# A listed order for all engine queues, one GpSimd operation moved, and idle products in the early gaps of TensorE

## The chip, the cores and the metric

One core of one Trainium2 chip runs the whole program. The metric is the device time of one execution in microseconds (us), the median of three timed runs; less is better. One more execution was recorded by the hardware profiler; every row below is from it.

## The reference

Gated linear attention feeds a channel-mixing layer, all in float32. Per batch (4) and head (8), over 768 steps, with 48 values per head:

```python
for t in range(S):
    state = alpha[:, :, t, :, None] * state + np.einsum('bhd,bhe->bhde', k[:, :, t], v[:, :, t])
    y[:, :, t] = np.einsum('bhd,bhde->bhe', q[:, :, t], state)
x = y.transpose(0, 2, 1, 3).reshape(B, S, H * D)          # 4 x 768 x 384
xk = mu_k * x + (1.0 - mu_k) * x_prev                     # x_prev: one step earlier
xr = mu_r * x + (1.0 - mu_r) * x_prev
k = np.maximum(xk @ w_k, 0.0)                             # 384 -> 1024
v = k * k @ w_v                                           # 1024 -> 384
r = 1.0 / (1.0 + np.exp(-(xr @ w_r)))
return (r * v)
```

## The kernel before

**Attention.** The 4 x 768 steps are cut into 24 chunks of 128, two chunks to a group `a` (12 groups). For a group, VectorE (DVE) forms running products of alpha with three scans `forth{a}.p`, multiplies q by them (`qP`), takes reciprocals (`turn`), runs three scans backwards (`back`) and multiplies k (`kP`). GpSimd (POOL) keeps the end values in between (`ends`: a copy to `pends`, a scaled copy to `pe`), and `turn` waits for them. For chunk `i`, TensorE (PE) transposes k (`trans`, tile `pt`), ScalarE (ACT) copies it out (`ht`), and PE multiplies: `enter{i}` (update of the state, scores) and `visit{i}` (outputs of the chunk), or, from `visit4` on, both in one job, `visit{i}` with the update and scores of chunk `i+1`. DVE masks the scores (`mask`) and advances the state (`state`), ACT and DVE move the outputs into `xt` (`leave`, `cross`).

**Channel mix.** Groups are joined to 7 column blocks `g` (two of 256 columns, five of 512). For each, the mix with the step before (`scale`, `blend`, `high`, `low`: a value is split into a rounded part and a remainder, so that three products in the fast float32 format give full accuracy), then on PE eight `up{g}.f` jobs of 9 matmuls, three `gate{g}.m`, and `down{g}.m.quarter`, four pieces of 6 matmuls for each of three output rows. ACT and DVE turn an up product into squares (`relu`, `square`, `whole`, `rest`).

**Weights** are loaded as packed words and split by ACT and DVE in the first 57 us: `top` (ACT, tile `tops` or `early`), `join` (DVE), `high` (ACT), `low` (DVE), for `k0` to `k3`, `r0`, `r1`, `v0` to `v3`. `down0.m.2` and `.3` need `v2` and `v3`.

**Order.** Everything that is added to the plan is a job with an engine, a cost in us and its needs. `Plan.order` tries 60 priority lists, keeps the shortest by its own costs, and the jobs are then issued in that order; each engine works its own queue strictly in that order. SyncE (SP) issues the transfers, and it too waits in its queue: a transfer whose data are not ready holds up those behind it. Three things lie outside the plan: 20 matmuls on zeros at the start, idle products (dummies) on zeros in front of the first real job of PE, and the operation `nu = 1 - mu` on POOL, issued ahead of all jobs. A dummy is one matmul of 112 columns, which the profile records as two.

```python
    todo = plan.order(sizes, ROUNDS)
    POOL.tensor_scalar(nu, mu, -1.0, 1.0, op0=ALU.mult, op1=ALU.add)
    at = WARMED
    cold = True
    for j in todo:
        if plan.eng[j] == "PE":
            if cold and at == WARMED:
                for i in range(int((plan.start[j] - at) / 0.19)):
```

Of the kernel before, what the change touches and what calls it, by code (L numbers as in the profile page):

```python
# [20 lines left out]
ALU = mybir.AluOpType  # L21
# [21 lines left out]
NT = 3  # L43
# [10 lines left out]
ROUNDS = 60  # L54
# [12 lines left out]
class Plan:  # L67
# [3 lines left out]
    LAG = {"PE": 0.25, "SP": 2.1, "DVE": 0.10, "ACT": 0.10, "POOL": 0.12}  # L71

    def __init__(self):
        self.eng, self.dur, self.fn, self.name, self.lag = [], [], [], [], []
        self.need = []
        self.first, self.users = {}, {}

    def add(self, eng, dur, fn, need=(), takes=(), uses=(), name="", lag=None):
# [3 lines left out]
        self.dur.append(dur)  # L82
        self.fn.append(fn)
# [31 lines left out]
    def run(self, pre, suc, key, free):  # L115

        n = len(self.eng)
        left = [len(d) for d in pre]
        ready = [0.0] * n
        start = [0.0] * n  # L120
        free = dict(free)
        wait = {e: [] for e in free}
        can = {e: [] for e in free}
        for j in range(n):
            if not left[j]:
                heapq.heappush(wait[self.eng[j]], (0.0, j))
        done = 0
        while done < n:
            best = None
            for e in free:  # L130
                if can[e]:
                    t = free[e]
                elif wait[e]:
                    t = max(free[e], wait[e][0][0])
                else:
                    continue
                if best is None or t < best[0]:
                    best = (t, e)
            t, e = best
            while wait[e] and wait[e][0][0] <= t:  # L140
                _, j = heapq.heappop(wait[e])
                heapq.heappush(can[e], (key[j], j))
            _, j = heapq.heappop(can[e])
            start[j] = t
            end = free[e] = t + self.dur[j]
            done += 1
            for k, lag in suc[j].items():
                ready[k] = max(ready[k], end + lag)
                left[k] -= 1
                if not left[k]:  # L150
                    heapq.heappush(wait[self.eng[k]], (ready[k], k))
        return start, max(s + d for s, d in zip(start, self.dur))

    def order(self, sizes, rounds):
# [3 lines left out]
        tail = [0.0] * n  # L158
        start, _ = self.run(pre, suc, list(range(n)), self.FREE)
        for j in sorted(range(n), key=lambda j: -start[j]):  # L160
            tail[j] = self.dur[j] + max((lag + tail[k] for k, lag in suc[j].items()), default=0.0)
        rng = random.Random(7)
        zero = {e: 0.0 for e in self.FREE}
        best = None
        key = [-x for x in tail]
        for r in range(rounds):
            start, span = self.run(pre, suc, key, self.FREE)
            if best is None or span < best[0]:
                best = (span, start, key)
            if r % 4 == 3:  # L170
                width = rng.choice((1.0, 2.0, 4.0, 8.0))
                key = [k + rng.uniform(-width, width) for k in best[2]]
            else:
                back, total = self.run(suc, pre, [-(s + d) for s, d in zip(start, self.dur)], zero)
                key = [total - b - d for b, d in zip(back, self.dur)]
        self.span, self.start = best[:2]
        return sorted(range(n), key=lambda j: (best[1][j], j))


# [1061 lines left out]
```

## Time and profile before

| | |
|---|---|
| median of 3 timed runs | 348.07 us (348.06 to 348.72) |
| profiled execution, its own time | 346.2 us |
| its span, first to last instruction | 344.5 us |
| busy: PE, DVE, ACT, POOL | 320.7, 221.1, 197.3, 20.4 us |
| mean granted clock of PE | 0.95 of full speed |

A timeline row gives start, length, engine, line, operation and tiles (out<-in), the count when like instructions follow each other, and in brackets how long the engine idled just before and what ended that. A clock of 1.00 is 2.4 GHz, 0.50 is 1.2 GHz. Matmuls are pipelined, so lengths of neighbouring PE rows overlap. Lines are those of the kernel before; in the changed kernel the same code stands 12 to 16 lines lower.

### The profile page before, as it was taken

The page shows a single profiled execution, that of the slowest core. Times are in us where ns is not written, and L with a number is a line of the kernel's source. Part 1 is how long each engine was busy: PE and PEld are TensorE (multiplying, and loading weights), DVE is VectorE, ACT ScalarE, POOL GpSimd, SP SyncE. Part 2 cuts the span into 40 slices and gives each one's busy share as a digit, 9 for nine tenths or more (in the row PEclk, how much of TensorE's full clock was granted, in tenths as well). Part 3 has the DMA queues.
Part 4 walks back from the last instruction along what each step waited for, and adds up shares of the span by engine and source line. Part 5 has one row for each costly group of instructions (what it writes and reads, how often), then busy time and mean ns, then how long its engine had stood idle before and what let it go on. Part 6 is the DMA issues. An engine that isn't in the chain of part 4 may idle for free.

```text
span 344.5 us, 10124 instructions
## 1 busy us (share of the span) xinstructions
PE 320.7 (93%) x4345; PEld 273.4 (79%) x4345; DVE 221.1 (64%) x421; ACT 197.3 (57%) x367; POOL 20.4 (6%) x60
## 2 busy tenths in 40 slices
PE   8546599999899999999999999999999999999992
PEld 8445599999798888888888888888888888888781
DVE  4979899896899537599337698264795212933010
ACT  4547799395378933199823299712398611987100
POOL 6100001020001002010001100000000000000000
PEclk9755599999999999999999999999999999999997
DMA  7797675324542035432035422043400001100011
GB/s 280 274 335 256 216 230 154 104 74 125 173 123 71 1 108 142 143 87 62 0 107 147 144 85 58 0 118 91 148 32 12 2 13 44 63 0 1 3 61 38
DMA packets 17204, 35.54 MB, mean 103 GB/s; under 512 B 3584, under 2 KB 7808, under 8 KB 17152
## 3 DMA queue, kind: packets, MB, share of 16 engines
q1 hardware_dynamic: 17008, 34.81, 33.0%
q8 instruction: 36, 0.59, 0.7%
q14 instruction: 16, 0.13, 0.1%
q10 hardware_dynamic: 144, 0.00, 0.0%
HBM read 26.55 MB, written 4.72 MB: 91 GB/s over the span
## 4 chain that ended last, share of the span: by engine, by line
PE 70%; DMA 9%; DVE 9%; ACT 7%; issue 2%; POOL 1%; SPq 1%; ACTq 0%; DVEq 0%
PE pm L847 24%; PE pm L810 24%; PE pm L835 9%; PE yu L485 3%; PE yu L513 3%; DMA xt<-xt 2%; PE sp L497 2%; DMA early<-wk_p 2%; DMA al<-al_p 2%; DMA mu<-mu_p 2%; PE pt L468 2%; ACT x L790 2%; DVE pp L409 2%; PE sp L535 1%; PE yu L535 1%
## 5 line engine op out<-in xcount | busy, mean ns | idle before, releaser
L810 PE MATMUL pm<-xkh,wkh 128*128 128x512 f32 (+1 forms) x168 | 43.8, 370 | 1.5 <-ACT xkh L796 1.5
L810 PE MATMUL pm<-xkh,wkl 128*128 128x512 f32 (+1 forms) x168 | 42.8, 364 | 0.0
L810 PE MATMUL pm<-xkl,wkh 128*128 128x512 f32 (+1 forms) x168 | 42.6, 362 | 0.0
L847 PE MATMUL pm<-kb,wvh 128*128 128x512 f32 x120 | 42.1, 402 | 0.0
L790 ACT ACTIVATE x<-xt,mu 128x512 f32<-128x512 f32 (+1 forms) x42 | 25.2, 654 | 28.0 <-DMA xt<-xt 28.0
L847 PE MATMUL pm<-kha,wvh 128*128 128x512 f32 (+1 forms) x108 | 38.4, 355 | 0.0
L847 PE MATMUL pm<-kla,wvh 128*128 128x512 f32 (+1 forms) x108 | 37.0, 342 | 0.0
L847 PE MATMUL pm<-kha,wvl 128*128 128x512 f32 (+1 forms) x108 | 36.8, 341 | 0.0
L810 PEld LDWEIGHTS pm<-xkh,wkh 128*128 128x128 f32 x168 | 29.6, 193 | 6.8 <-ACT xkh L796 1.7
L810 PEld LDWEIGHTS pm<-xkh,wkl 128*128 128x128 f32 x168 | 29.9, 193 | 5.0
L816 ACT ACTIVATE r<-pm 128x512 f32<-128x512 f32 (+1 forms) x56 | 29.5, 530 | 7.6 <-PE pm L810 6.9
L810 PEld LDWEIGHTS pm<-xkl,wkh 128*128 128x128 f32 x168 | 29.8, 192 | 4.9
L822 ACT ACTIVATE k<-r 128x512 f32<-128x512 f32 (+1 forms) x56 | 31.5, 565 | 3.2 <-DVE kla L825 2.3
L825 DVE TENSOR_TENSOR kb<-k,kb 128x512 fp32r<-128x512 f32 x20 | 13.9, 693 | 24.2 <-ACT kb L819 12.9
L969 DVE TENSOR_TENSOR sig<-pm,sig 128x512 f32<-128x512 f32 (+1 forms) x21 | 12.8, 613 | 24.8 <-PE pm L847 24.6
L582 DVE TENSOR_TENSOR am<-sp,mask 128x512 f32<-128x512 f32 x24 | 16.4, 683 | 17.8 <-PE sp L497 17.8
L793 DVE SCALAR_TENSOR_TENSOR x<-xt,nu,x 128x512 f32<-128x512 f32 (+1 forms) x42 | 26.4, 665 | 1.5 <-ACT x L790 1.3
L560 ACT COPY xt<-yu 112x512 f32<-112x512 f32 x24 | 13.9, 580 | 23.3 <-PE yu L535 21.8
L649 ACT COPY ht<-pt 128x384 f32<-128x384 f32 x24 | 16.3, 677 | 19.1 <-PE pt L468 18.9
L847 PEld LDWEIGHTS pm<-kb,wvh 128*128 128x128 f32 x120 | 22.6, 188 | 5.0
L365 DVE TENSOR_TENSOR_SCAN pp<-al,tiny 128x256 f32<-128x256 f32 x36 | 22.8, 675 | 4.8 <-DMA al<-al_p 4.8
L409 DVE TENSOR_TENSOR_SCAN pp<-al,pp 128x255 f32<-128x255 f32 x36 | 25.2, 736 | 0.5 <-DVE pp L402 0.2
(90 smaller groups left out, 604.6 us busy)
## 6 DMA issues: line engine op xcount, KB each, us to landing
v<-v_p SPq DMA_DIRECT2D x12, 400.0 KB, 4.6
al<-al_p SPq DMA_DIRECT2D x12, 384.0 KB, 3.3
q<-q_p SPq DMA_DIRECT2D x12, 384.0 KB, 3.8
k<-k_p SPq DMA_DIRECT2D x12, 384.0 KB, 3.7
out<-sig SPq DMA_DIRECT2D x15, 256.0 KB, 2.1
early<-wk_p SPq DMA_DIRECT2D x4, 768.0 KB, 6.3
early<-wv_p SPq DMA_DIRECT2D x4, 768.0 KB, 4.5
q<-q SPq DMA_DIRECT2D x24, 48.0 KB, 2.2
```

The lines of the kernel that those rows point to most:

```text
L365: DVE.tensor_tensor_scan(view(a, pps)[:, p], view(a, als)[:, p], tiny.to_broadcast([128, n]), initial=START, op0=ALU.mult, op1=ALU.max,)
L409: DVE.tensor_tensor_scan(pp[:, p, 0 : n - 1][:, ::-1], x, x, initial=pp[:, p, n - 1 : n], op0=ALU.mult, op1=ALU.bypass,)
L560: ACT.copy(x[:R].rearrange("r i (s t) -> r i s t", s=2), yu[:R, :, : NP * HC].rearrange("r s (i t) -> r i s t", i=NP),)
L582: DVE.tensor_tensor(ams[i % 2], sp[:, :, : NP * HC].rearrange("c j (p t) -> c j p t", p=NP), mask.unsqueeze(1).unsqueeze(1).to_broadcast([ ...
L649: ACT.copy(hts[(i + 1) % 2].rearrange("t (r i) -> t i r", i=NT), pt)
L790: ACT.activation(x, now, AF.Copy, scale=mu[:, i, t : t + 1])
L793: DVE.scalar_tensor_tensor(x, prev, nu[:, i, t : t + 1], x, op0=ALU.mult, op1=ALU.add)
L810: PE.matmul(pk, w[:, t, cols], x[:, t], start=part == 0 and t == 0, stop=part == 2 and t == NT - 1,)
L816: ACT.activation(r, pk, AF.Relu)
L822: ACT.activation(k2, r, AF.Square)
L835: PE.matmul(pg, w[t // 2][:, t % 2, cols], x[:, t], start=part == 0 and t == 0, stop=part == 2 and t == NT - 1,)
L847: PE.matmul(pv, w[f // 2][:, f % 2, cols], x, start=f == 0 and i == 0, stop=f == NF - 1 and i == 2,)
```

## The change

`Plan.order` and its search are gone. A list of all 1,079 jobs, `ORDER`, stands in the source, and `Plan.follow` issues them in it, working out a start for each from the costs; costs were altered too (SP's jobs now have an issue time and a separate transfer time), but they now set only those starts. `nu` becomes a job on POOL that needs `ends0`; it stands behind `ends1` in the list. Dummies fill 0.6 of each gap that the worked-out starts leave on PE until the first job that takes the third accumulator (`up0.2`): besides the 13 in front of `trans0`, as before, now 38 more, in this order: 5, 3, 6, 4, 3, 2 before `trans1`, `enter0`, `visit0`, `enter1`, `trans2`, `trans3`, then 5, 5 and 5 before `enter2`, `visit2` and `enter3`.

```diff
-ROUNDS = 60
+FILL = 0.6
+ISSUE = 0.42
...
-    def order(self, sizes, rounds):
+    def follow(self, sizes, order):
+
         self.rings(sizes)
         pre, suc = self.links()
         n = len(self.eng)
...
+        for j in todo:
+            t = self.FREE[self.eng[j]]
+            if j in behind:
+                t = max(t, start[behind[j]] + self.dur[behind[j]])
+            start[j] = max([t, *(end[i] + lag for i, lag in pre[j].items())])
+            end[j] = start[j] + self.dur[j]
+            if self.moved[j]:
+                end[j] = max(end[j], end[behind[j]] if j in behind else 0.0) + self.moved[j]
...
+        place = {j: i for i, j in enumerate(order)}
+        return sorted(range(n), key=lambda j: (start[j], place[j]))
...
+ORDER = """
+0 2 213 18 1 218 4 5 6 7 9 8 10 15 12 214 13 20 22 11 3 215 14 216 24 16 263 219 217 264 220 223 19 268 25 221
...
+"""
...
-            jb = add("DVE", dve(n) + 0.05, b_, need=[js], uses=[("x", xi), ("xt", g)], name=f"blend {tag}{g}.{t}")
+            jb = add("DVE", dve(n) + 0.05, b_, need=[js, weighed], uses=[("x", xi), ("xt", g)], name=f"blend {tag}{g}.{t}")
...
+    weighed = add(
+        "POOL", 0.3, lambda: POOL.tensor_scalar(nu, mu, -1.0, 1.0, op0=ALU.mult, op1=ALU.add),
+        need=[rescale[0][0]], name="nu",
+    )
...
-    todo = plan.order(sizes, ROUNDS)
-    POOL.tensor_scalar(nu, mu, -1.0, 1.0, op0=ALU.mult, op1=ALU.add)
+    todo = plan.follow(sizes, [int(x) for x in ORDER.split()])
...
-            if cold and at == WARMED:
-                for i in range(int((plan.start[j] - at) / 0.19)):
+            if cold:
+                gap = plan.start[j] - at
+                for i in range(int((gap if at == WARMED else FILL * gap) / 0.2)):
```

On DVE, around `kP1` (the product into `k_102`), before. The join of weight `k3` (`early<-early,tops_171`) stands ahead of it:

```order
L764 TENSOR_TENSOR wkl_156<-early,wkh_152 128x768
L570 TENSOR_TENSOR xt_178<-xt_178,sp 112x2x64 x2
L752 SCALAR_TENSOR_TENSOR early<-early,tops_171 128x768
L393 TENSOR_TENSOR k_102<-k_102,pp_100 128x768
L613 TENSOR_TENSOR st_132<-st_131,yu 112x192
L616 TENSOR_TENSOR st_133<-st_132,yu 112x192
L618 TENSOR_TENSOR st_133<-st_133,pe_143 112x192
L582 TENSOR_TENSOR am_177<-sp,mask 128x512
```

The same place on DVE in the changed kernel:

```order
L776 TENSOR_TENSOR wkl_156<-early,wkh_152 128x768
L408 TENSOR_TENSOR k_102<-k_102,pp_100 128x768
L628 TENSOR_TENSOR st_132<-st_131,yu 112x192
L631 TENSOR_TENSOR st_133<-st_132,yu 112x192
L633 TENSOR_TENSOR st_133<-st_133,pe_143 112x192
L597 TENSOR_TENSOR am_177<-sp,mask 128x512
L380 SCALAR_TENSOR_TENSOR pp_99<-al_97,tiny 128x256 x3
L764 SCALAR_TENSOR_TENSOR early<-early,tops_171 128x768
L585 TENSOR_TENSOR xt_178<-xt_178,sp 112x2x64 x2
```

The join moved behind `kP1`, `state1`, `mask1` and three scans of group 2, still ahead of `cross1` (`xt_178`).

On SP, before, around the loads of group 4 (`k_101` and `q_103` are its k and q). The gather of `pe` stands ahead of the load of q:

```order
L327 DMA k_101<-k_p 128x768
L444 DMA pe_143<-pe_143 48x1x1 x2
L327 DMA q_103<-q_p 128x768
L350 DMA v_105<-v_p 128x800
L579 DMA xt_178<-xt_178 16x3x256 x2
```

The same place on SP in the changed kernel:

```order
L341 DMA k_101<-k_p 128x768
L986 DMA out<-sig_195 128x256
L341 DMA q_103<-q_p 128x768
L364 DMA v_105<-v_p 128x800
L459 DMA pe_143<-pe_143 48x1x1 x2
L594 DMA xt_178<-xt_178 16x3x256 x2
```

The loads of q and v moved ahead of the gather, and a store came in between.

On PE, before, at the third piece of the first down product (`wvh_160` is weight `v2`). The piece follows the second one (`wvh_159`) at once:

```order
L847 MATMUL pm_72<-kha,wvh_159 128x256
L847 MATMUL pm_72<-kha,wvl_163 128x256
L847 MATMUL pm_72<-kla,wvh_159 128x256
L847 MATMUL pm_72<-kha,wvh_160 128x256
L847 MATMUL pm_72<-kha,wvl_164 128x256
```

The same place on PE in the changed kernel, where the last rows of `visit4` stand ahead of the piece:

```order
L550 MATMUL sp<-q_103,st_132 64x64
L550 MATMUL sp<-q_103,st_131 64x64
L512 MATMUL sp<-q_103,k_101 64x64 x16
L859 MATMUL pm_72<-kha,wvh_160 128x256
L859 MATMUL pm_72<-kha,wvl_164 128x256
```

`enter4` and the whole of `visit4` moved from within and behind the third down product to ahead of this piece.

## Rows read from the trace of the kernel before

**Rows 1.** Stretch, length; busy (count) by engine; PEclk; DMA share; GB/s.
```profile
57.50:338.50 281.00, 278.61 (x3643) 234.61 (x3641) 171.35 (x333) 157.77 (x293) 11.96 (x24) 1.00 0.25 72
```

**Rows 2.** Timeline of PE at 89 us: start, length, instruction, [idle before].
```profile
89.69 0.77 PE L485 MATMUL yu<-v,ht 64*64 64x48 f32 x29 [1.68 <-ACT ht L649]
```

**Rows 3.** The same columns as in 1, VectorE alone.
```profile
8.40:57.04 48.64, 45.02 (x83) 0.68 0.79 257
```

**Rows 4.** Timeline of VectorE up to 57 us.
```profile
8.40 0.18 DVE L402 RECIPROCAL pp<-pp 128x3 f32<-128x3 f32 x1 [1.37 <-POOL pe L383]
...
14.17 1.84 DVE L365 TENSOR_TENSOR_SCAN pp<-al,tiny 128x256 f32<-128x256 f32 x3
...
16.78 0.95 DVE L393 TENSOR_TENSOR q<-q,pp 128x768 f32<-128x768 f32 x1
17.65 0.34 DVE L613 TENSOR_TENSOR st<-st,yu 112x192 f32<-112x192 f32 x1
...
18.30 0.68 DVE L582 TENSOR_TENSOR am<-sp,mask 128x512 f32<-128x512 f32 x1
...
25.12 0.96 DVE L752 SCALAR_TENSOR_TENSOR early<-early,tops 128x768 uint32<-128x768 uint32 x1 [1.29 <-ACT tops L744]
...
31.87 0.48 DVE L570 TENSOR_TENSOR xt<-xt,sp 112x128 f32<-112x128 f32 x2
...
37.27 0.48 DVE L793 SCALAR_TENSOR_TENSOR x<-xt,nu,x 128x256 f32<-128x256 f32 x1 [0.93 <-ACT x L790]
...
54.55 0.76 DVE L825 TENSOR_TENSOR kla<-k,kha 128x256 fp32r<-128x256 f32 x2
55.22 1.82 DVE L764 TENSOR_TENSOR wvl<-early,wvh 128x768 fp32r<-128x768 f32 x2
```

**Rows 5.** Timeline of GpSimd.
```profile
7.68 0.20 POOL L1051 TENSOR_SCALAR nu<-mu 128x6 f32<-128x6 f32 x1 [1.62 <-DMA mu<-mu_p]
```

**Rows 6.** Timeline of PE up to 69 us.
```profile
7.40 2.72 PE L1058 MATMUL pm<-zero 112*112 112x112 f32 x26
12.66 0.72 PE L468 MATMUL pt<-ident,k 128*128 128x128 f32 x3 [2.53 <-DVE k L393]
...
15.11 0.97 PE L485 MATMUL yu<-v,ht 64*64 64x48 f32 x30
...
15.95 1.09 PE L497 MATMUL sp<-q,k 48*64 48x64 f32 x30
...
39.91 1.01 PE L810 MATMUL pm<-xkh,wkh 128*128 128x256 f32 x3 [1.53 <-ACT xkh L796]
...
57.48 0.28 PE L847 MATMUL pm<-kha,wvh 128*128 128x256 f32 x1
...
62.80 0.79 PE L485 MATMUL yu<-v,ht 64*64 64x48 f32 x30
...
64.09 0.39 PE L847 MATMUL pm<-kha,wvh 128*128 128x256 f32 x1
...
66.72 0.77 PE L485 MATMUL yu<-v,ht 64*64 64x48 f32 x15
...
68.86 0.55 PE L468 MATMUL pt<-ident,k 128*128 128x128 f32 x3
```

**Rows 7.** Stretches as in 1, for the clock of PE.
```profile
12.00:13.00 1.00, 0.34 (x3) 0.35 (x3) 1.00 (x2) 1.00 (x2) 0.00 (x0) 0.92 0.64 234
28.65:33.50 4.85, 4.85 (x131) 4.12 (x131) 4.49 (x9) 3.06 (x5) 0.48 (x1) 0.50 0.85 251
88.00:89.69 1.69, 0.01 (x1) 0.00 (x1) 1.62 (x7) 1.64 (x4) 0.00 (x0) 1.00 0.80 177
```

**Rows 8.** SyncE from 60 to 95 us: its waits, then its timeline.
```profile
SPq L444 <- POOL pe L383: 5.6, 1, 5.6
...
77.47 0.53 SPq L327 DMA_DIRECT2D q<-q_p  x1
```

**Rows 9.** Chain that ended last: start, length, engine, tile, line, count.
```profile
202.08 16.69 PE pm L810 x72
```

More of the change, by code (lines that the diff above doesn't have):

```diff
@@ L70, with add @@
     FREE = {"SP": 0.8, "DVE": 1.6, "ACT": 2.4, "POOL": 3.6, "PE": 1.6}
-    LAG = {"PE": 0.25, "SP": 2.1, "DVE": 0.10, "ACT": 0.10, "POOL": 0.12}
+    LAG = {"PE": 0.25, "SP": 1.9, "DVE": 0.10, "ACT": 0.10, "POOL": 0.12}
     def __init__(self):
         self.eng, self.dur, self.fn, self.name, self.lag = [], [], [], [], []
-        self.need = []
+        self.need, self.moved = [], []
         self.first, self.users = {}, {}
-    def add(self, eng, dur, fn, need=(), takes=(), uses=(), name="", lag=None):
+    def add(self, eng, dur, fn, need=(), takes=(), uses=(), name="", lag=None, moved=0.0):
         j = len(self.eng)
@@ L113, in links @@
         return pre, suc
[L115 to L152, printed above, removed]
-    def order(self, sizes, rounds):
+    def follow(self, sizes, order):
         self.rings(sizes)
@@ L157, in order @@
         n = len(self.eng)
[L158 to L177, printed above, removed]
+        assert sorted(order) == list(range(n))
+        last, behind, ahead = {}, {}, {}
+        for j in order:
+            e = self.eng[j]
+            if e in last:
+                behind[j] = last[e]
+                ahead[last[e]] = j
+            last[e] = j
+        left = [len(d) + (j in behind) for j, d in enumerate(pre)]
+        self.start = start = [0.0] * n
+        end = [0.0] * n
+        todo = [j for j in range(n) if not left[j]]
+        for j in todo:
[6 more added lines that the diff above has]
+                end[j] = max(end[j], end[behind[j]] if j in behind else 0.0) + self.moved[j]
+            for k in (*suc[j], *([ahead[j]] if j in ahead else [])):
+                left[k] -= 1
+                if not left[k]:
+                    todo.append(k)
+        assert len(todo) == n
+        self.span = max(end)
+        place = {j: i for i, j in enumerate(order)}
+        return sorted(range(n), key=lambda j: (start[j], place[j]))
 def mm(n):
-    return 0.013 + n / 2400.0 if n > 128 else 0.068
+    return n / 2240.0
 def dve(n, psum=False):
@@ L339, in fetch @@
             tag = x + str(half)
-            ids = [add("SP", move(128 * NT * n * 4), one, takes=[(x, a)], name=f"load {x}{a}")]
+            ids = [add("SP", ISSUE, one, moved=move(128 * NT * n * 4), takes=[(x, a)], name=f"load {x}{a}")]
             if direct:
-                ids.append(add("SP", 0.5, extra, takes=[(x, a)], name=f"load {x}{a} again"))
+                ids.append(add("SP", 2 * ISSUE, extra, moved=0.5, takes=[(x, a)], name=f"load {x}{a} again"))
             took[x] = ids
@@ L449, in attention_inputs @@
                 rescale[a].append(
-                    add("SP", 0.1, small, need=[end], uses=[("pe", a)], name=f"gather pe{a}")
+                    add("SP", 1.25, small, moved=0.05, need=[end], uses=[("pe", a)], name=f"gather pe{a}")
                 )
@@ L715, in attention_products @@
                     mv = add(
-                        "SP", 0.2, lambda a=a: spread(a), need=done[a], uses=[("xt", slot_of[a])], name=f"spread{a}"
+                        "SP", 1.25, lambda a=a: spread(a), moved=0.35, need=done[a], uses=[("xt", slot_of[a])], name=f"spread{a}"
                     )
```

26 lines of the change are left out of this document (12 added, 14 removed), and 39 rows, old and new, of the table ORDER.

## The prediction

> **What bounds the kernel now.** I read the stretches first, then each engine in order of time, then the waits, and the chain last. From 57.5 us on TensorE (PE) is busy 278.61 of 281.00 us [rows 1]: there the time is matmul work, and an order can only win back the 2.39 us in which PE idles. 1.68 of them are one wait at 88 us, for a transposed tile `ht` [rows 2]. What else can be won lies before 57 us.
>
> There VectorE (DVE) is the limit: from 8.40 to 57.04 us it is busy 45.02 of 48.64 us [rows 3], so it idles 3.62 us. Three waits make up most of what matters. At 8.40 its reciprocal has waited 1.37 us for GpSimd (POOL) [rows 4], because POOL had stood 1.62 us in `nu` until the transfer of `mu` landed [rows 5]. At 25.12 a join waited 1.29 us for ScalarE's (ACT) tile `tops`, and at 37.27 a blend 0.93 us for `x` [rows 4]. DVE's last weight remainders (`low v2`, `low v3`, line 764) run from 55.22 to 57.04 [rows 4]; the third piece of the first down product, `down0.0.2`, follows on PE at 57.48 [rows 6]. I take this point, M, as the milestone. Whatever PE has done beyond the old list when it passes M, and whatever time M moves, is the gain; behind it both kernels have the same matmuls to do.
>
> **The change, part by part, against the profile's own span of 344.5 us.**
>
> *`nu` behind `ends0`.* It removes the wait at 8.40. The reciprocal then needs the end values, which POOL takes while DVE multiplies `q` (0.95 us for such a product [rows 4]), so nearly all of 1.37 is saved: **1.3 us** for DVE. `nu` is then due only at the first blend, at 37.27 in the old trace, some 20 us after its new place behind `ends1`: no cost.
>
> *The new DVE list up to `low v3`.* Comparing the two lists, nothing leaves it and these jobs are moved in front: `forth3.1`, `forth3.2`, `rest0.6`, `rest0.7`, `cross3`, `qP3`, `turn3`, `state4`, `mask4`. Prices [rows 4]: two scans at 1.84/3 = 0.61 make 1.22; two `rest` 0.67 (54.55 to 55.22); `cross` 0.48; `qP` 0.87 (16.78 to 17.65); `state` 0.65 (17.65 to 18.30); `mask` 0.68 less the overlap, 0.60; the reciprocal 0.1. Sum **4.6 us** more ahead of M.
>
> *DVE's idle time.* The 1.29 us wait was a join that stood in front of `kP1` while its weight was still in transfer; the join now stands behind `kP1`, `mask1` and three scans, and its load now stands ahead of the gather of `pe` and the load of `v` that it was behind. The 0.93 us wait sat behind the chain `kP1`, `mask1`, `cross1`, transfer of `xt`; that chain now starts some 4 us earlier (1.3 from `nu`, 1.29 from the wait, 0.9 from the join itself, and `cross1` has two jobs less ahead of it), and two other jobs, `low r0` and `qP2`, stand before the blend. I take both as gone, 2.2 us; the bounds are 0 and all 3.62 us. So `low v3` ends at 57.04 - 1.3 + 4.6 - 2.2 = 58.1, `low v2` 0.9 earlier, and **M = 57.2** (bounds 55.8 and 59.4).
>
> *What PE has done at M.* The old list has none of chunk 4's products there, the new one all: `enter4`, 62.80 to 64.09, and `visit4`, 66.72 to 68.86 [rows 6], together 1.29 + 2.14 = **3.43 us**. Can PE be at M by 57.2? From its first up product (39.91) to M it needed 17.57 us [rows 6]; less `enter3`, which now comes earlier (1.29), plus 3.43, it needs 19.7, and 1.9 less if the first two up products don't run at half clock. So up products that begin by 39.4 do, and the chain above lets them begin near 36. PE waits at M, not DVE. Gain at M: 57.48 - 57.2 + 3.43 = **3.7 us**.
>
> *Dummies in the early gaps.* 38 more of the 112-column products. At full clock 13 of them take 2.72 us [rows 6], 0.21 each, 7.9 us in all, within gaps that PE has anyway. As DVE decides M, the clock itself gives nothing that is not counted; they cost only if they run at half clock (below). Before, the clock was 0.92 in the microsecond from 12 to 13 and then half: it fell after the dummies had ended at 10.12 and PE had idled 2.53 us to 12.66 [rows 6, 7]. That gap shrinks by the 1.3 us, and the next ones hold dummies. Through the idle 1.68 us at 88 us the clock stayed at 1.00 [rows 7]. I take it that the clock holds.
>
> Here a rule is weighed. PE was busy 4.85 of 4.85 us from 28.65 to 33.50, with `visit` and `enter` products alone, and the clock stayed at 0.50 (1.2 GHz) [rows 7]. The Trainium skill ("TensorE: Matmul & The Clock Gate", What's actually happening) says that the gate is set by how busy PE has recently been: half rate by default, released by sustained activity. By it this stretch should have brought the clock back, and the new, fuller early stage would be safe; by the row, the small products alone do not bring a lost clock back, so it hangs on the dummies. By the rule the sum stands; by the row a fall that happens lasts to the first up products, which is the second rival.
>
> *SyncE's queue.* Before, the gather of `pe` stood in SP's queue ahead of the load of `q` for group 4 and waited 5.6 us for POOL; the load went out at 77.47 [rows 8]. That delay runs through `qP4`, `kP4` and the next loads into the 1.68 us wait of PE at 89.69 [rows 2]. Now the loads of `q` and `v` stand ahead of that gather, so I count **1.7 us** back. Against it, visits 9 to 11 are moved up by 10 to 20 us, into the up products of group 2, and need loads and gathers sooner. The trace of before has no such place; the bound below is 0, the bound above as large as the old waits, 2.4. I take 0.4, near the low end, because each visit still has more than 10 us of other products between it and its predecessor's release of the buffers.
>
> Sum: 3.7 + 1.7 - 0.4 = **5.0 us**. The profiled span goes from 344.5 to 339.5, that execution's own time from 346.2 to 341.2. The median of the three timed runs, 348.07, lies 1.87 above the profiled one; I carry that over: **343.1 us**.
>
> **The rivals.**
>
> *DVE wins back no idle time.* New waits replace the two named ones, since a denser list in one order is more easily held up. Then M is 59.4, the gain there 57.48 - 59.4 + 3.43 = 1.5, and if the later waits also come back as large as before, the time is 348.07 - 1.5 = 346.6. For it: ACT and the weight loads are no faster than before, and the extra jobs depend on ACT's results.
>
> *The clock falls anyway; slower.* Place: the gaps between 11 and 36 us. From `trans0`, now near 11.3, to the end of `visit2` PE has four transposes at 0.72, 33 dummies at twice 0.21, and six `enter` and `visit` blocks at 1.93 (15.11 to 17.04 at half clock) [rows 6]: 2.9 + 13.9 + 11.6 = 28.4, so `visit2` ends at 39.7; five dummies (2.1) and `enter3` (1.9) put the first up product at 43.7 and M at 43.7 + 19.7 = 63.4. Gain: 57.48 - 63.4 + 3.43 + 1.3 = -1.2, that is 349.3. It decides where M passes 62.2. For it: the dummies fill only part of each gap. Against it: the dummies are spread over all of the gaps, and none of the idle stretches left is as long as the 2.53 us after which the clock fell.
>
> *TensorE's long stretch is not full.* Weight loads are busy only 234.61 of its 281.00 us [rows 1]; if order could close a tenth of the other 46.4, the time would be 4.6 less than forecast, 338.5. Against it: 72 matmuls of 512 columns take 16.69 us, 0.232 each, in one unbroken piece of the chain [rows 9], and no order changes their number. The Trainium skill ("Perfetto Trace Analysis", Identifying the Most-Contended Engine) calls matmul busy time a poor measure of headroom and the weight loads' share a good one; by that rule this rival holds, and the trace agrees only with the share, not with the room.
>
> **How the numbers follow.** The forecast, 343.1, gets 0.62; its own range is 341 to 345. DVE without its idle time, or half of it, near 346.6: 0.20. The clock falls, near 349.3: 0.12, of which a third stays within 0.2%. PE's stretch shrinks: 0.02; something else, either way: 0.04. 0.2% (0.7 us) is about what a measurement of this kernel can tell from no change. Faster by more than that takes the first two, the fourth and some of the rest: 0.83; within it 0.07; slower 0.10. The low end of the range is the forecast with all DVE idle gone (1.4 less) and no new waits and no old ones (1.1 less): 340.6. The high end takes in the first rival with something above it: 347.0.
>
> **What would show it.** Right: DVE's first reciprocal near 7.1; `kP1` ending near 23, ahead of the join that it stood behind; the first up product near 36, at clock 1.00; `visit4` before M, PE idle for 2 us or so in front of `down0.0.2` near 57; no wait of SP for POOL ahead of the load of group 4's `q`; PE unbroken from there to the end, and 512-column matmuls at 0.232. Wrong: clock 0.50 in the records between 13 and 36 us, M above 60, or a new wait of more than 2 us behind M, at a transpose or a visit that comes too early.

## The result, and the profile after

The changed kernel takes 343.77 us (median of 4 executions, 343.34 to 344.42), the kernel before beside it 348.39 us (348.06 to 348.83): a ratio of 0.986, 95% interval 0.983 to 0.989. A second comparison on another chip, told below, gave 342.57 us and a ratio of 0.983 (0.980 to 0.986). All ten executions together have a median of 343.1 us, the number that was forecast; the kernel before has 348.6 over 78 executions in all comparisons. Four more of its executions, beside e5 to e10, ran in a slower state and are left out of every median and ratio here. The gain is 5.5 us. But the two profiles stand only 2.3 us apart (own times 346.2 and 343.89, spans 344.5 and 342.2), so part of the forecast's way to its number must be wrong. The lines of the profile after are read with that in mind.

The page of the profile after, TensorE's clock in 40 slices of 8.6 us:

```profile
PEclk9999999699999999999999999999999999999997
```

The early slices are at 9, where [rows 7] had 0.50 (a second profile, a11, has an early fall, see there); the eighth slice, from 60 to 68 us, shows a 6. The stretches say the same (length; busy of PE, PE's weight loads, DVE, ACT, POOL; PEclk; DMA share; GB/s):

```profile
10.00:36.00 26.00, 20.55 (x545) 18.16 (x544) 25.25 (x48) 16.79 (x27) 4.45 (x6) 1.00 0.86 284
36.00:57.00 21.00, 18.91 (x355) 17.93 (x354) 19.03 (x39) 17.30 (x41) 1.13 (x2) 1.00 0.69 211
57.00:65.00 8.00, 6.25 (x28) 5.95 (x29) 7.61 (x14) 5.20 (x11) 0.00 (x0) 0.57 0.44 117
65.00:110.00 45.00, 45.00 (x896) 42.51 (x896) 38.17 (x84) 29.04 (x66) 2.75 (x8) 1.00 0.45 127
110.00:330.00 220.00, 220.00 (x2517) 180.62 (x2516) 122.93 (x229) 123.26 (x217) 3.20 (x15) 1.00 0.22 62
```

The clock is at 1.00 up to 57 us, falls to 0.57 on average over 57 to 65, and PE has no idle time at all from 65 to 330 us, where it had 2.39 us in the long stretch before [rows 1]. So what is still lost is lost around the milestone M. The timeline of PE there:

```profile
36.63 0.28 PE L822 MATMUL pm<-xkh,wkh 128*128 128x256 f32 x1 [0.91 <-ACT x L802]
...
58.05 0.48 PE L859 MATMUL pm<-kha,wvh 128*128 128x256 f32 x1 [2.33 <-ACT wvh L772]
59.23 0.58 PE L859 MATMUL pm<-kha,wvl 128*128 128x256 f32 x1 [0.70 <-DVE wvl L776]
...
64.31 0.41 PE L859 MATMUL pm<-kha,wvh 128*128 128x256 f32 x1
64.52 0.41 PE L859 MATMUL pm<-kha,wvl 128*128 128x256 f32 x1
...
65.23 0.28 PE L859 MATMUL pm<-kla,wvh 128*128 128x256 f32 x1
65.35 0.28 PE L859 MATMUL pm<-kha,wvh 128*128 128x256 f32 x1
```

The up products begin by 36.63, at the full clock. `visit4` ends at 55.73, and PE then stands for 2.33 us until the third piece of down product 0 can start, does one product, and stands 0.70 us more for `low v2`. Behind that its products come 0.21 us apart, in place of 0.12: the clock has gone to 0.50 (1.2 GHz), and it is back at 65 us. What PE waits for is read from ACT and then from DVE:

```profile
52.56 1.07 ACT L756 ACTIVATE early<-early 128x768 f16<-128x768 bf16 x1
56.20 1.06 ACT L756 ACTIVATE tops<-early 128x768 f16<-128x768 bf16 x1 [2.56 <-DMA early<-wv_p]
57.12 0.87 ACT L772 ACTIVATE wvh<-early 128x768 fp32r<-128x768 f32 x1
```

```profile
7.71 0.18 DVE L417 RECIPROCAL pp<-pp 128x3 f32<-128x3 f32 x1 [0.40 <-POOL pe L398]
...
57.29 0.96 DVE L764 SCALAR_TENSOR_TENSOR early<-early,tops 128x768 uint32<-128x768 uint32 x1 [1.53 <-ACT tops L756]
...
58.25 1.95 DVE L776 TENSOR_TENSOR wvl<-early,wvh 128x768 fp32r<-128x768 f32 x2
```

`top v3` on ACT waits 2.56 us for the transfer of weight v3. Behind it in ACT's queue stands `high v2`, for which nothing is missing, and on DVE `join v3` (57.29) stands ahead of `low v2`. So the transfer of v3 also delays v2, which PE needs first. `low v2` and `low v3` (58.25, two of them) end at 60.20; 58.1 was forecast.

That transfer is itself tied to DVE. The packed weights have two buffers in turn, so the load of v3 needs the buffer of v1, which `low v1` on DVE reads last. It ends at 49.68 (first row below), and the load, the second of the two in the second row, goes out at 49.71:

```profile
48.72 0.96 DVE L776 TENSOR_TENSOR wvl<-early,wvh 128x768 fp32r<-128x768 f32 x1
```

```profile
47.62 2.42 SPq L751 DMA_DIRECT2D early<-wv_p  x2
```

DVE's time from its first reciprocal to the end of `low v3`:

```profile
7.71:60.20 52.49, 49.39 (x94) 0.98 0.78 254
```

It idles 52.49 - 49.39 = 3.10 us, against 3.62 before [rows 3]. The first reciprocal, at 7.71, is 0.69 earlier than in [rows 4], and it still waits for POOL, where the copy of the end values takes longer than its 0.19 us before. The copies of groups 0 and 1 on POOL, and DVE's product of `q` beside the first:

```profile
6.38 0.98 POOL L396 COPY pends<-pp 128x6 f32<-128x6 f32 x1 [0.31 <-DVE pp L380]
...
15.24 1.70 POOL L396 COPY pends<-pp 128x6 f32<-128x6 f32 x1 [7.56 <-DVE pp L380]
```

```profile
6.35 0.96 DVE L408 TENSOR_TENSOR q<-q,pp 128x768 f32<-128x768 f32 x1
```

The first copy ends at 7.36, 0.05 us behind DVE's product, which ends at 7.31. The last section comes back to this.

On SP's queue the loads of group 4 now go out at 71 us and the gather of `pe` stands behind them, without the wait of [rows 8]:

```profile
71.11 0.33 SPq L341 DMA_DIRECT2D q<-q_p  x1
72.86 1.21 SPq L459 DMA_DIRECT2D pe<-pe  x2
```

### The profile page after: what moved, and what is told of

Read it like the earlier page. It is cut to its first block, busy times and chain, and to the rows that moved or that the text cites. A ratio compares the mean times of both kernels' runs of the same rounds, so it can differ in the third digit from the quotient of the medians.

```text
span 342.2 us, 10261 instructions
## 1 busy us (share of the span) xinstructions
PE 325.7 (95%) x4421; PEld 278.7 (81%) x4421; DVE 220.4 (64%) x421; ACT 196.2 (57%) x367; POOL 17.9 (5%) x60
## 5 line engine op out<-in xcount | busy, mean ns | idle before, releaser
L859 PE MATMUL pm<-kha,wvh 128*128 128x512 f32 (+1 forms) x108 | 39.4, 365 | 2.3 <-ACT wvh L772 2.3
L859 PE MATMUL pm<-kb,wvh 128*128 128x512 f32 x120 | 41.3, 401 | 0.0
L859 PE MATMUL pm<-kha,wvl 128*128 128x512 f32 (+1 forms) x108 | 38.3, 355 | 0.7 <-DVE wvl L776 0.7
L859 PE MATMUL pm<-kla,wvh 128*128 128x512 f32 (+1 forms) x108 | 38.2, 353 | 0.0
L822 PEld LDWEIGHTS pm<-xkh,wkh 128*128 128x128 f32 x168 | 28.6, 188 | 4.9
L859 PEld LDWEIGHTS pm<-kha,wvh 128*128 128x128 f32 x108 | 21.6, 200 | 5.0 <-ACT wvh L772 2.5
L837 DVE TENSOR_TENSOR kla<-k,kha 128x512 fp32r<-128x512 f32 (+1 forms) x36 | 20.0, 566 | 8.3 <-ACT k L834 4.1
L380 DVE TENSOR_TENSOR_SCAN pp<-al,tiny 128x256 f32<-128x256 f32 x36 | 23.5, 679 | 2.4 <-POOL st L277 2.4
```

The source lines that it names most:

```text
L380: DVE.tensor_tensor_scan(view(a, pps)[:, p], view(a, als)[:, p], tiny.to_broadcast([128, n]), initial=START, op0=ALU.mult, op1=ALU.max,)
L822: PE.matmul(pk, w[:, t, cols], x[:, t], start=part == 0 and t == 0, stop=part == 2 and t == NT - 1,)
L837: DVE.tensor_tensor(lo, k2, hi.bitcast(F32), op=ALU.subtract)
L859: PE.matmul(pv, w[f // 2][:, f % 2, cols], x, start=f == 0 and i == 0, stop=f == NF - 1 and i == 2,)
```

## The experiments

Four comparisons with the kernel before, each on one chip; its median was 348.55 us beside e1 to e4, 348.51 beside e5 to e10, 348.62 beside a11, e13 and e14, and 349.17 beside e15. The changed kernel stood beside it in the first comparison (343.77) and in a11's (342.57) alone, 1.2 us apart. So medians of different comparisons can be set beside each other to about 1 us. "The changed kernel" is 343.1 us, the median of its ten executions.

### e1: the kernel before, once more

No edit.

> The kernel before, unchanged, so that its executions can be compared among themselves. Its profiled execution took 346.2 us (span 344.5, clock 0.950), its timed ones 348.06 to 348.83. Theory A: the timed ones lose 2 us or so on PE at half clock that the profiled one does not; then their spans are near 346.5 and their clocks below 0.950. Theory B: the difference lies around the span; then the spans are 344.5 and the clocks 0.950 in all.

Measured: 348.44 us (346.44 to 349.82, 12 executions), ratio 1.000 (0.998 to 1.002). Its profile (own time 348.3, span 346.5) answers why the first profile of before, 346.2, lies so low: only one of the 78 executions was at or under that. Timeline of PE, then two stretches:

```profile
90.68 0.85 PE L485 MATMUL yu<-v,ht 64*64 64x48 f32 x29 [1.78 <-ACT ht L649]
```

```profile
90.68:92.00 1.32, 1.32 (x58) 1.32 (x62) 1.32 (x3) 0.16 (x1) 0.00 (x0) 0.70 0.26 102
92.00:94.00 2.00, 2.00 (x82) 2.00 (x74) 0.57 (x2) 0.59 (x1) 0.00 (x0) 0.50 0.03 8
94.00:96.00 2.00, 2.00 (x20) 1.88 (x17) 1.36 (x5) 0.31 (x1) 0.00 (x0) 0.85 0.76 208
```

M is at 57.98, 0.5 us later than in [rows 6]. The wait for `ht` is the one of [rows 2], 1.78 us in place of 1.68; but here the clock falls behind it: 1.32 us at 0.70, 2.00 at 0.50 and 2.00 at 0.85 lose 0.4 + 1.0 + 0.3 = 1.7 us. Together 2.2, where the spans differ by 2.0. The other two profiles of the old order fit: e2's (own time 346.7) keeps the clock there, e5's (348.17) loses it behind another wait.

### e2: `nu` behind `ends1`, in the old order

```diff
-    POOL.tensor_scalar(nu, mu, -1.0, 1.0, op0=ALU.mult, op1=ALU.add)
...
+        if plan.name[j] == "ends1":
+            POOL.tensor_scalar(nu, mu, -1.0, 1.0, op0=ALU.mult, op1=ALU.add)
```

> The kernel before with nu alone moved, issued behind ends1. Theory A (VectorE's list decides when the third down piece can start): the wait of 1.37 us goes, VectorE is 1.3 us ahead from 8.4 us on, and up to 1.3 us comes off the time. Theory B (the transfers of the weights decide): VectorE loses the lead again where it waits for weight k3 near 25 us, and the time stays within 0.4 us.

Measured: 347.25 us (344.91 to 349.5, 12), ratio 0.997 (0.994 to 1.000): 1.2 us, if only just: the interval goes from 0.1 to 2.2. Its first reciprocal comes at 7.67, against 8.69 in e1's profile, 1.0 us earlier, and of that 0.5 is left where `low v3` ends (57.77 against 58.28). So the gain agrees with the term of 1.3 us, but the interval is too wide to bear out its size.

### e3: the changed kernel without the early dummies

```diff
-FILL = 0.6
+FILL = 0.0
```

> The changed kernel without the 38 added dummies. Theory A (VectorE's list decides the milestone, the clock hardly counts): the clock falls to 0.50 from 13 us to the first up products, which cost 1.9 us more, but PE idles 3.2 us ahead of the third down piece and absorbs most of it; time within 0.7 us of the changed kernel's 343.8. Theory B (the clock is what the change gains): the six enter and visit blocks cost 0.6 us each and the up products 1.9 more, 4 to 6 us slower, near 348.

Measured: 345.93 us (343.73 to 348.12, 12), ratio 0.993 (0.990 to 0.995): 2.8 us slower than the changed kernel. A stretch (columns as above), and PE's timeline:

```profile
10.00:36.00 26.00, 15.54 (x426) 13.04 (x426) 24.11 (x43) 15.57 (x25) 3.01 (x6) 0.55 0.82 262
```

```profile
61.62 0.58 PE L859 MATMUL pm<-kha,wvl 128*128 128x256 f32 x1 [0.69 <-DVE wvl L776]
```

DVE's waits from 10 to 57 us (us in total, times, longest):

```profile
DVE early L764 <- ACT tops L756: 0.9, 2, 0.5
DVE xt L585 <- ACT xt L575: 0.6, 1, 0.6
DVE kla L837 <- ACT kha L831: 0.6, 1, 0.6
DVE early L764 <- ACT early L756: 0.5, 1, 0.5
```

Without dummies the early clock is 0.55 in place of 1.00 in the profile after, DVE is busy 1.1 us less in that stretch, and the third piece passes 2.4 us later than with them (59.23). DVE's waits over 10 to 57 us come to 2.6 us, and 1.2 of them are for outputs and squares that come from PE through ACT; in the profile after they come to 0.9, all for weights. So the dummies are worth something like 2.8 us in this order (2.4 to 3.3 by the ratios).

### e4: the changed kernel with `nu` at its old place

```diff
-        "POOL", 0.3, lambda: POOL.tensor_scalar(nu, mu, -1.0, 1.0, op0=ALU.mult, op1=ALU.add),
+        "POOL", 0.3, lambda: None,
...
+    POOL.tensor_scalar(nu, mu, -1.0, 1.0, op0=ALU.mult, op1=ALU.add)
```

> The changed kernel with nu back ahead of all jobs on GpSimd. Theory A (VectorE's list decides): the reciprocal waits 1.4 us again instead of 0.4, all behind it is 1.0 us later, 1.0 us slower (344.8). Theory B (weight v3's transfer decides the third and fourth down pieces): the 1.0 us vanishes in VectorE's wait of 1.5 us for weight v3, time within 0.4 us of 343.8.

Measured: 344.0 us (341.72 to 344.95, 6), ratio 0.988 (0.985 to 0.990), 0.9 us above the changed kernel, with intervals that overlap, so the move of `nu` can't be told from nothing here. Its first reciprocal comes at 8.53 us, 0.82 later than in the profile after, but `low v3` ends at 60.45, only 0.25 later, as DVE's wait for `tops` is 1.07 us in place of 1.53. Against a11, the other profile of the changed kernel, it is not so: there the reciprocal comes at 7.63, the wait is 1.03 and `low v3` ends at 59.66, so 0.79 of 0.90 us comes through. In the profile after, 6.5 us lie between the issue of the load of v3 and the start of `top v3`, in a11 and here 6.0. So whether DVE's later start is lost in that wait is not settled. The profiled execution, the fastest of the six, shows something else as well. PE waited 1.88 + 0.80 us at M and kept its clock, by its timeline and the stretch behind it:

```profile
58.28 0.39 PE L859 MATMUL pm<-kha,wvh 128*128 128x256 f32 x1 [1.88 <-ACT wvh L772]
59.47 0.39 PE L859 MATMUL pm<-kha,wvl 128*128 128x256 f32 x1 [0.80 <-DVE wvl L776]
```

```profile
57.00:65.00 8.00, 5.85 (x45) 5.45 (x46) 7.37 (x14) 5.43 (x12) 0.00 (x0) 1.00 0.43 112
```

### e5: the old order with the dummies

```diff
-            if cold and at == WARMED:
-                for i in range(int((plan.start[j] - at) / 0.19)):
+            if cold:
+                gap = plan.start[j] - at
+                for i in range(int(gap / 0.19 if at == WARMED else 0.6 * gap / 0.2)):
```

> The kernel before, in its own order, with dummies in 0.6 of its own early gaps as well. Theory A (VectorE's list decides the milestone): the clock holds near 1.00 to 40 us, the first up products run at full clock, but the third down piece cannot start before VectorE's last weight remainders at 57 us; the time falls by no more than 0.5 us. Theory B (the clock is what the change gains): 2 to 4 us faster.

Measured: 348.59 us (347.59 to 350.61, 12), ratio 1.002 (1.000 to 1.005). In the old order the same dummies give nothing. DVE's waits from 10 to 57 us show why: 4.5 us, for weights and for ACT's scaled `x`, and none for what PE makes. A faster PE helps only the new order, where such waits appear (e3).

### e6: twelve dummies in the wait at M

```diff
+            if plan.name[j] == "down0.0.2":
+                for i in range(12):
+                    PE.matmul(pms[0][:R, :R], zero, zero, start=True, stop=True)
```

> The changed kernel with 12 more dummies on PE between visit4 and the third down piece, in the accumulator that is free there. In the changed kernel the clock fell at 58.6 us, after PE had idled since 55.7, and stayed at 0.50 to 64.9. Theory A: with the gap filled the clock stays at 1.00 and the products from 59.2 to 64.9 take half the time, 2.8 us faster than the changed kernel, near 341.0. Theory B: behind the gap something else sets the end (VectorE, the next group's mix), and less than 1 us comes off.

Measured: 342.1 us (340.9 to 344.31, 6), ratio 0.983 (0.978 to 0.988), 1.0 us under the changed kernel, with intervals that overlap. PE's timeline:

```profile
56.55 2.61 PE L1077 MATMUL pm<-zero 112*112 112x112 f32 x24
...
60.27 0.39 PE L859 MATMUL pm<-kha,wvl 128*128 128x256 f32 x1 [0.76 <-DVE wvl L776]
```

PE passes M a microsecond later than in the profile after (`low v2` came later in this execution), the products behind it run at the full clock, and the span is 341.0, 1.2 less.

### e9: the gather of group 4 back ahead of the loads

```diff
-313 76 555 551 604 546 608 78 547 93 320 73 560 540 74 317 314 565 75 77 315 79 561 570 316 321 319 88 609 566
+313 76 555 551 604 546 608 78 547 93 320 88 73 560 540 74 317 314 565 75 77 315 79 561 570 316 321 319 609 566
```

(88 is the gather of `pe`, 73 and 74 are the loads of `q` and `v` of group 4.)

> The changed kernel with one step of the transfer queue put back: the gather of pe for group 4 ahead of the loads of q and v, as before. Theory A: the loads wait for GpSimd again, the chain through qP4 and kP4 is late, and PE waits some 1.7 us again at a transposed tile: 1 to 2.5 us slower than the changed kernel's 343.8. Theory B: the delay is hidden, since this list has other work there; within 0.5 us.

Measured: 345.73 us (343.72 to 347.53, 12), ratio 0.992 (0.989 to 0.996), 2.6 us slower than the changed kernel. SP's waits, and PE's timeline behind M:

```profile
SPq L459 <- POOL xt L570: 2.8, 1, 2.8
```

```profile
81.08 0.55 PE L483 MATMUL pt<-ident,k 128*128 128x128 f32 x3 [1.33 <-DVE k L408]
83.18 0.55 PE L483 MATMUL pt<-ident,k 128*128 128x128 f32 x3 [0.53 <-ACT ht L661]
```

The gather waits 2.8 us for POOL (1.1 in the profile after, with the loads ahead of it), and 1.86 us of idle time come back on PE, at the transposes. That is near the price that the forecast gave the place in SP's queue, 1.7 us. The rest of the 2.6 us is within what two comparisons can differ by.

### e10: `visit4` behind the down pieces

```diff
-509 58 505 531 254 511 306 60 506 61 259 255 70 62 256 56 260 68 63 261 257 552 262 532 307 57 64 533 65 536
+509 58 505 531 254 511 60 506 61 259 255 70 62 256 56 260 68 63 261 257 552 262 532 307 57 64 533 306 65 536
```

(306 is `visit4`, 532 and 533 are the third and fourth piece of down 0.)

> The changed kernel with visit4 alone put back behind the first down product. Theory A: the third down piece still waits for VectorE near 59 us, PE idles 2.1 us longer ahead of it and does visit4 (2.14 us) behind: 2.1 us slower than 343.8, near 345.9. Theory B: PE makes the time up later because something behind sets the pace; within 0.7 us.

Measured: 345.26 us (343.9 to 347.66, 12), ratio 0.992 (0.989 to 0.995), 2.2 us slower. PE's timeline:

```profile
57.23 0.58 PE L859 MATMUL pm<-kha,wvh 128*128 128x256 f32 x1 [4.15 <-ACT wvh L772]
```

The wait at M is 4.15 us in place of 2.33: most of what `visit4` (2.14) filled is idle. Work that PE has done when it passes M counts in full, as the forecast took it.

### a11, e13 and e14: the changed kernel, and two orders around M

a11 is the changed kernel without an edit.

> The changed kernel itself, once more, on the chip on which the next two run, so that they and it stand beside the same runs of the kernel before. Theory A (the gain between medians is that of the first comparison): ratio 0.985 to 0.989, 343.5 to 344.7 us. Theory B (the first comparison was lucky by the spread between executions, and the gain is the 2.3 us between the two profiles): ratio about 0.993, 346 us. PE's two waits in front of the third piece of down product 0 again 2.3 + 0.7 us, within 0.5, and the granted clock 0.50 behind them.

e13 moves two pieces of down 1 (536, 537), which need only v0 and v1, ahead of the third piece of down 0 (532), and takes the need that tied them to its fourth piece (533) out of the plan:

```diff
-509 58 505 531 254 511 306 60 506 61 259 255 70 62 256 56 260 68 63 261 257 552 262 532 307 57 64 533 65 536
-556 548 66 537 529 67 538 89 539 553 69 308 311 542 557 534 558 543 309 312 535 544 72 310 554 545 549 559 550
+509 58 505 531 254 511 306 60 506 61 259 255 70 62 256 56 260 68 63 261 257 552 262 536 537 532 307 57 64 533 65
+556 548 66 529 67 538 89 539 553 69 308 311 542 557 534 558 543 309 312 535 544 72 310 554 545 549 559 550
...
+    plan.need[536].remove(533)
```

> The changed kernel with the first two pieces of down product 1, which need only weights v0 and v1, moved ahead of the third piece of down product 0: PE has 12 products (1.4 us at the full clock) in the place where it waited 2.33 + 0.70 us. Theory A (the wait and the half clock behind it cost what they show in the profile): 1.4 us of the wait is filled, about 1.6 us is left of it; 1.4 us less than the changed kernel beside it, and up to 2.8 us more if the clock now holds: 339.6 to 342.4 us if that one is at 343.8. Theory B (behind this place DVE sets the time, which the change of PE's order does not touch: visit 5 takes its masks from DVE at 65.5 us, and starts at 69.3 us now): the gain is lost again in new waits ahead of visit 5, 0 to 0.5 us.

e14 moves all that doesn't need v3 ahead of what does, on PE, ACT (256 `high v2` and 529, a sigmoid, ahead of 259 `top v3`) and DVE (257 `low v2` ahead of 260 `join v3`):

```diff
-509 58 505 531 254 511 306 60 506 61 259 255 70 62 256 56 260 68 63 261 257 552 262 532 307 57 64 533 65 536
+509 58 505 531 254 511 306 60 506 61 256 529 259 255 70 62 56 257 260 68 63 261 552 262 536 537 532 307 57 64 538 542 543 544 533 65
...
+    plan.need[536].remove(533)
+    plan.need[542].remove(539)
```

> The changed kernel with the place in front of weight v3 reordered as a whole. ScalarE: high v2 and the sigmoid of gate 2 ahead of top v3, which waits 2.56 us for its transfer. DVE: low v2 ahead of join v3. PE: behind visit 4 come down 1's first two pieces, down 0's third, down 1's third, down 2's first three, and only then the three last pieces, which need v3: 42 products (4.9 us) between 55.7 and 60.65 us, when low v3 (60.2 us) is there. Theory A: no wait of over 0.3 us between 55.7 and 63 us and the clock at 1.00 throughout, so down 2 ends near 62.8 in place of 69.2 us; then visit 5 must wait for DVE's masks and states (65.5 us), so that 3.8 us of the 6.4 are kept: about 340 us if the changed kernel beside it is at 343.8. Theory B (the next stretch, group 1's inputs on DVE and ScalarE, takes more of it): waits ahead of the first up product of group 1 as well, gain 1 to 2 us.

Measured, all beside the same kernel before: a11 342.57 us (342.23 to 343.22, 6), ratio 0.983 (0.980 to 0.986); e13 341.32 us (340.29 to 341.49, 6), ratio 0.979 (0.975 to 0.982); e14 341.96 us (340.3 to 344.93, 6), ratio 0.983 (0.978 to 0.987). PE's timeline in a11 at M, where the clock is at 0.50 from 59 to 62.3 us:

```profile
57.55 0.38 PE L859 MATMUL pm<-kha,wvh 128*128 128x256 f32 x1 [1.84 <-ACT wvh L772]
58.73 0.43 PE L859 MATMUL pm<-kha,wvl 128*128 128x256 f32 x1 [0.80 <-DVE wvl L776]
```

a11 again, earlier: a stretch, PE's first transposes and DVE's wait behind them:

```profile
10.00:36.00 26.00, 21.67 (x537) 19.78 (x537) 24.49 (x45) 16.26 (x25) 4.36 (x6) 0.87 0.84 275
```

```profile
11.74 0.87 PE L483 MATMUL pt<-ident,k 128*128 128x128 f32 x3 [2.41 <-DVE k L408]
```

```profile
18.17 0.69 DVE L597 TENSOR_TENSOR am<-sp,mask 128x512 f32<-128x512 f32 x1 [1.36 <-PE sp L512]
```

e13 at M, with the clock at 1.00 from 57 us on:

```profile
57.68 0.38 PE L859 MATMUL pm<-kha,wvh 128*128 128x256 f32 x1 [0.75 <-ACT wvh L772]
58.87 0.38 PE L859 MATMUL pm<-kha,wvl 128*128 128x256 f32 x1 [0.81 <-DVE wvl L776]
62.83 0.55 PE L483 MATMUL pt<-ident,k 128*128 128x128 f32 x3 [0.66 <-DVE k L408]
```

e14, where nothing waits at M and the clock stays at 1.00:

```profile
65.83 0.74 PE L500 MATMUL yu<-v,ht 64*64 64x48 f32 x29 [1.88 <-ACT xkh L808]
```

a11 settles the gain between medians: it isn't the 2.3 us of the two profiles. It also shows an early fall of the clock that the profile after doesn't have: 0.50 from 12 to 17 us and 1.00 again by 18. It fell towards the end of an idle stretch of 2.41 us, in place of 1.22, as the first dummies ended at 9.33 in place of 10.60. DVE then waits 1.36 us for PE's scores. e15 has the same fall, e4, e9, e10 and e13 one of 3 to 4 us. e13 gives 1.25 us beside a11, and its slowest execution is under a11's fastest; its moved products are 12 at 0.1175, 1.4 us, and its clock held at M besides, where a11 lost 1.6 us; part of the two together is lost again, 0.66 us of it in the wait at 62.83. e14 takes all waiting from M, and has 1.88 us of it again in front of `visit5`, which starts at 65.83, against 67.63 in a11. So 1.8 us of some 4 were kept at that point, and by the end fewer: the spans are 339.7 and 340.6. Behind M, then, DVE and ACT decide as soon as PE is 2 us earlier. The second of the two theories comes nearer, and the gain in the medians, 0.6 us with intervals that overlap, is under both. Why e14's executions spread over 4.6 us isn't settled. e13 is the fastest of the kernels tried with all its work in place.

### e15: only a quarter of weight v3 transferred

```diff
+            m = n // 4 if (key, f) == ("v", 3) else n
-            SP.dma_start(raw.bitcast(U16)[:, 1 : 4 * n + 1], src[:, at : at + n].bitcast(U16))
+            SP.dma_start(raw.bitcast(U16)[:, 1 : 4 * m + 1], src[:, at : at + m].bitcast(U16))
```

> The changed kernel with only the first quarter of weight v3 transferred (192 of 768 KB); its split runs on what the buffer holds. Three quarters of v3 are so left out of the data, and no operation of any engine is. It takes away the one wait to which the missed DVE idle time is put down: top v3 waiting 2.05 to 2.56 us for the transfer. Theory A (the transfer of v3 holds top v3, behind which high v2 stands, and so low v2 and low v3): top v3 starts within 0.3 us of top v2's end, near 53.7 us, low v2 and low v3 end near 58.7 instead of 59.7 to 60.2, the third piece of down 0 has its low part near 57.7 instead of 58.7 to 59.2, and the clock is likelier to hold; ratio to the kernel before 0.976 to 0.981, where the changed kernel had 0.983 and 0.986. Theory B (the queues of DVE and ScalarE themselves end there, whenever v3 comes): low v3 still ends at 59.7 us or later, ratio 0.983 to 0.986.

Measured: 341.64 us (341.15 to 342.64, 5), ratio 0.980 (0.977 to 0.983), 1.5 us under the changed kernel, with an interval that overlaps a11's. Timeline of ACT, then of PE (its lines stand one lower):

```profile
53.84 1.07 ACT L757 ACTIVATE early<-early 128x768 f16<-128x768 bf16 x1
54.78 1.08 ACT L757 ACTIVATE tops<-early 128x768 f16<-128x768 bf16 x1
```

```profile
57.19 0.38 PE L860 MATMUL pm<-kha,wvh 128*128 128x256 f32 x1 [0.19 <-ACT wvh L773]
58.89 0.56 PE L860 MATMUL pm<-kha,wvl 128*128 128x256 f32 x1 [1.32 <-DVE wvl L777]
```

With the transfer short, `top v3` runs right behind `top v2`, and `high v2` no longer makes PE wait. From the start of `top v2` to the second product of the third piece it takes 58.89 - 53.84 = 5.05 us, against 59.23 - 52.56 = 6.67 in the profile after and 6.18 in a11: the transfer costs 1.1 to 1.6 us there. But `top v2` itself came 1.28 us later in this execution, so the times that were expected of M were missed, and the clock fell again. Against the profile after, the waits put that down mainly to the 1.30 us that DVE waits at 18.25 for PE's scores, with the clock at 0.50 from 11.5 to 17.5 us, as in a11. `low v3` ends at 59.84, which was the sign of theory B; the ratio is in the range of theory A. So it is shown that the wait for v3 holds up `high v2`; what it is worth at M and in the end time is not settled, as the intervals overlap.

## Why the prediction was right, point by point

The number was right; its parts were right in kind, two were mis-sized, and two falls of the clock and one gain were left out. All in us; the columns are the two profiles of the changed kernel (a11's span is 340.6), against the one of before with its span of 344.5.

| step | forecast | profile after | a11 |
|---|---|---|---|
| `nu`: first reciprocal earlier than 8.40 | 1.3 | 0.69 | 0.77 |
| DVE's added work up to `low v3` | 4.6 | 4.37 | 4.24 |
| DVE's idle time won back | 2.2 | 0.52 | 0.85 |
| `low v3` ends | 58.1 | 60.20 | 59.66 |
| gain at M | 3.7 | 1.8 | 2.3 |
| half clock behind M | 0 | -2.7 | -1.6 |
| idle time and waits behind M | 1.3 | 2.4 | 2.4 |
| sum | 5.0 | 1.5 | 3.1 |
| difference of the spans | 5.0 | 2.3 | 3.9 |

The 0.8 us between the last two rows is in no step, in either column. About half of it can be found: `trans5`, the transposes for chunk 5, also moved ahead of M (before at 58.85, 0.24 us to the next product; after at 44.07), and neither the forecast nor this table counts it; and the tail behind the last product is 0.15 us shorter (6.67 before, 6.52 after).

**The added work on DVE** held within 0.4 us, and e10 bears out that PE's extra products at M count in full.

**`nu`** gave 0.69 to 0.77 of its 1.3 us. The step that was off is that POOL takes the end values while DVE multiplies `q`: its copy took 0.98 us and ended 0.05 behind that product, so the reciprocal still waited 0.40. The wait itself fell by 0.97; the product ahead of it ended at 7.31 in the profile after, and at 8.40 - 1.37 = 7.03 in the first profile. How much of this reaches the end is open in the new order (e4) and known only to lie between 0.1 and 2.2 us in the old one (e2).

**DVE's idle time won back**, 2.2, is the term that was sized wrong. The two named waits did go: DVE's waits from 10 to 57 us fell from 3.2 to 0.9 us. The term took no account of a new one at its end: the 1.53 us in front of `join v3`, with `top v3` on ACT waiting for the transfer of v3 (e15). In a11 there is a second one, 1.36 us for PE's scores behind the early fall of the clock. The first rival said as much, that a denser list is more easily held up, but put M's delay together with a return of the later waits, and those did not come back.

**The gain at M**: M is 59.23, inside its bounds of 55.8 to 59.4, with one product done before: 57.48 - 59.11 + 3.43 = 1.8, by the forecast's own formula.

**The clock.** It was taken to hold early. In the profile after it did; in a11 and five more of the nine profiles of this order with its dummies it fell between 11 and 14 us, which was named as a sign of being wrong. By 18 us it was back, over PE's dummies, transposes and `enter0`, so the first up products ran at 1.00. Its price at M is not known: in a11 DVE waited 1.36 us for it, and still a11 passes M 0.5 us before the profile after (58.73 and 59.23). That a fall lasts to the first up products, as the forecast had it from [rows 7], did not hold with the dummies in between; without them (e3) the mean was 0.55 up to 36 us. The fall that cost most was not looked for: the forecast named the idle 2 us at M as a sign that it was right, and there the clock fell. In the profile after 27 products from 59.23 to 65.11 take 5.88 us where 0.1175 apart would be 3.2: 2.7 us lost. In a11 17 products from 58.73 to 62.36 take 3.63 in place of 2.0: 1.6 lost. The half clock ends within an unbroken run of 256-column products; that activity releases it, as the Trainium skill ("TensorE: Matmul & The Clock Gate", What's actually happening) has it, agrees with these rows. "The clock itself gives nothing not counted" was wrong too: the dummies are worth 2.8 us in the new order (e3).

**Behind M** all 2.39 us of idle time [rows 1] went, and no new wait came: 2.4 in place of 1.7 - 0.4. e9 shows the SP term alone, 1.86 us of idle time.

**The carried 1.87 us.** The profiled span was forecast as 339.5 and came out as 342.2 and 340.6; the median was right because the forecast carried over that before's median lay 1.87 above its profiled execution, while the changed kernel's own profiles lie at theirs (343.89 to 343.77, 342.3 to 342.57). Two errors cancelled. But carrying it was not mere luck: e1 shows what the difference was in the kernel before, a fall of the clock behind the wait for `ht`, which the first profile didn't have. That most executions have it is argued from the times, not shown. This wait is gone in the changed kernel, and with it a loss of 1.7 us that no row of the first profile shows.

**The rivals.** DVE without its idle time came nearer the truth at M than the forecast did (59.4 there, 59.23 and 58.73 measured), and missed the end. The clock's early fall happened in a11 and was over by 18 us, so the price of 349.3, with half clock up to the first up products, did not come up; e3, at 0.55 from 10 to 36 us but without the dummies that the rival ran at half speed, has M at 61.62 and 345.93 us, so that price itself was not tried. The chances for a faster kernel, 0.62, 0.20 and 0.02, already make 0.84, where the forecast says 0.83. TensorE's long stretch: from 110 to 330 us PE is busy 220.00 of 220.00 with weight loads at 180.62, the same 82% as before, and nothing was won there.

What stays open: the other half of the 0.8 us; how often the clock falls at M in executions without a profile; and how e14's time divides.

## What to carry to other kernels

Where a transfer is the last thing to land, look at what stands behind the instruction that waits for it on each in-order queue: here v2's conversion stood behind v3's, and PE needed v2 first; and the load of v3 could go out only when DVE had freed its buffer. An idle gap on TensorE is priced with what the clock may lose behind it, and products that need only what is already there can fill it (e13: 1.4 us of real work moved, 1.25 us gained). Before a sum is made against one profiled execution, see where that execution lies among the timed ones, and ask which waits cost more in the others. Take a second profile of the changed kernel too: here one alone would have said that the clock holds early.

## What the runs showed of the hardware

The same wait may or may not cost the clock. Behind 1.88 + 0.80 us at M it held (e4), behind 1.84 + 0.80 it fell (a11), and behind 0.19 + 1.32 it fell too (e15); in the old order it held behind 1.68 us [rows 2] and 1.72 (e2), and fell behind 1.78 (e1) and 1.46 (e5). Where it fell at M, it stayed at 0.50 for 3.4 us (a11, e15) to 6.8 us (e3, e9, e10). The falls in a11, e1 and the profile after cost 1.6, 1.7 and 2.7 us, and the executions of the kernel before spread over 4.9 us (345.47 to 350.4).

The same copy on POOL took from 0.19 to 1.71 us, and what DVE did at the time goes with it. Beside the product of `q` it took 0.98 and ended 0.05 us behind that product (profile after). For group 1 it took 1.70 (15.24 to 16.94) beside a remainder and the product of `q` on DVE, which ends at 16.89; the kernel before shows the same there, 1.71 us, ending 0.06 behind the product. Where DVE stood idle, as at 8 us in the kernel before and in e4, it took 0.19:

```profile
7.99 0.19 POOL L396 COPY pends<-pp 128x6 f32<-128x6 f32 x1
```

So `nu` ahead of it is not what made the copy short there: DVE was already done. No run moves the product of `q` away from the copy, so this is read from the times alone.
